# Attention and a top-1 mixture of experts on one core: one ring of PSUM banks, and gates, counts, flag and forms moved to other places

## The chip, the core and the metric

The kernel runs on one NeuronCore of a Trainium2 chip. The core has five engines with a program each: PE (TensorE, matmuls and transposes), DVE (VectorE), ACT (ScalarE), POOL (GpSimd) and SP (which issues transfers). [...] PE writes its results to PSUM, [...]; DVE and ACT read them from there. PE's clock can be throttled, and the profile shows the share that was granted. The metric is the device time of one execution in microseconds. Before the change it is 605.97 us, the median of three runs (602.70 to 607.75).

## What is computed

The reference joins two blocks. The first is attention with a band of `n_local` = 96 keys and `n_global` = 8 keys that every query sees, with a linear bias (4 sequences, 8 heads, 768 positions, 64 numbers per head). The second routes each of the 3072 rows of 512 numbers to one of eight experts:

```python
scores = scale * q @ k.T + bias(h, dist)        # bias = -slope[h] * distance
a = softmax(where(is_global | is_local, scores, -1e9))
x = (a @ v) as (B*S, H*D)                       # 3072 x 512
logits = x @ w_gate                             # 8 experts
expert_idx = argmax(logits)
gate_w = softmax(logits)[expert_idx]
for e in range(8):
    xe = x[expert_idx == e]
    out[expert_idx == e] = gate_w * (relu(xe @ w1[e]) @ w2[e])
```

All data are float32.

## The kernel before

**Attention** runs over 24 blocks of 128 queries (n), six to a sequence (i = n mod 6). It is software-pipelined: in step n the kernel makes the scores of block n, the transposes of q and k for block n + 1, the exponentials of block n, the tokens of block n − 2 (transposes back, logits), and the values of block n − 1. Each engine runs its part in program order. PSUM pools are rings: a new tile has to wait until the engine that reads the old tile in its bank is done.

```python
ps_s = tile_pool(name="ps_s", bufs=2, PSUM)   # scores sp, two banks each
ps_t = tile_pool(name="ps_t", bufs=2, PSUM)   # transposes pt (of q, k) and px
ps_o = tile_pool(name="ps_o", bufs=1, PSUM)   # values po
ps_r = tile_pool(name="ps_r", bufs=1, PSUM)   # pr: sums, logits, counts

def values(n):
    po = ps_o.tile([P, NPAIR, P], F32, tag="o", name="po")
    ...                                        # L387: po <- v, p
    nc.scalar.copy(ots[n][:], po[:])           # L391
    pr = prs[n] = ps_r.tile([P, 4, P], F32, tag="r", name="pr")
    ...                                        # L398: sums, pr[:, 0] <- one_in, p
    ...                                        # L403: logits, pr[:, 0] <- gate_w, ot
    nc.scalar.copy(rs[:], pr[:, 0, :])         # L406

def tokens(n, rs):
    nc.tensor.transpose(pr[:, 1, :], rs[:], ident[:])          # L414
    px = ps_t.tile([P, NPAIR, P], F32, tag="t", name="px")
    for m in range(NPAIR):
        nc.tensor.transpose(px[:, m, :], ot[:, m, :], ident[:])  # L417
    ...        # DVE: den (L423), reciprocal (L425), lh (L428), lg (L431),
    ...        # and the row of the token, xr <- px (L434)
    ...        # at i == 5: choose(...)
```

At the end of a sequence `choose` finds the expert of each token, `gates` the weight, and `dispatch` counts the tokens per expert on PE, works out a row for each token on DVE, and scatters the tokens to DRAM with POOL:

```python
def choose(...):
    ...                                        # top, sh, cand, oh on DVE
    nc.scalar.activation(sh[:], sh[:], AF.Exp)  # L185
    def gates():
        nc.vector.tensor_reduce(se[:], sh[:], AX.X, ALU.add)   # L189, + 4 more on DVE

def dispatch(pool, pr, rt, xr, oh):
    ...        # PE L201 to L207: counts in pr from oh (12 small bf16 matmuls)
    ...        # DVE L210 to L217: rk, slot, base_e from pr
    ...        # POOL L219: six scatters

for n in range(N + 1):
    scores(n); prep_q(n + 1); exps(n); prep_k(n + 1); mix_v(n + 1); load(n + 3)
    b, i = divmod(n - 2, NBLK)
    if n >= 2:
        if i == 0 and b:                       # n = 8, 14, 20
            gates()
            dispatch(pool, prs[n - 2][:, 2, :], rt, xr, oh)
        tokens(n - 2, rs.pop(n - 2))
    if n: rs[n - 1] = values(n - 1)
```

**Experts.** Two experts' first 128 tokens are started early (`up_s`, `down_s`: 128 tokens at a time), then eight passes take the rest of each expert's tokens, in a width that is only known at run time. The width is one of ten forms. Each pass is a `Switch` on a register: the engines load the registers once from the tile `form`, and jump to the code of the form. A `hint` on PE and ACT asks for the code of the next pass ahead of the jump.

```python
ex.begin(stack)                 # pools of the passes, over the space of attention
ex.up_s(0, 0)
dispatch(...); ex.up_s(0, 1)
ex.table(); ex.gathers(0); ex.x_in_s(1); ...   # table writes `form`
for half in range(2): ex.down_s(0, half)
for half in range(2): ex.up_s(1, half)
ex.fetch(2, nc.scalar)
ex.load_forms()                 # PE, ACT and DVE load `form` into registers
ex.hint(0)
ex.down_s(1, 0)
for t in range(TP): ex.x_in(0, t)
ex.x_meta(0); ex.down_s(1, 1)
ex.passes(judge)

def passes(self, judge):
    for e in range(E):
        for i in tc.Switch(index, len(WIDTHS), hint=f"pass{e}"):
            self.one_pass(e, WIDTHS[i], more)   # up L947, down L954, back L968
        ...                                     # fetch, gathers for later passes
        if e + 1 < E: self.hint(e + 1)
        s_ = e + NS
        parts = ...       # e <= 4: up_s, up_s, down_s, down_s of expert s_
                          # e == 5: up_s, up_s; e == 6: down_s, down_s; e == 7: none
        for fn in parts[:1] + [lambda: self.finish(e)] + parts[1:]: fn()
        if s_ == E: judge()
```

`judge` makes a flag (13 small operations on DVE, one matmul L1087, one more on DVE). After the passes every engine reads the flag and would start a general version of the program if the fast one did not apply; with this input it does not start.

Of the kernel before, what the change touches and what calls it, by code (L numbers as in the profile page):

```python
# [23 lines left out]
def kernel(  # L24
# [12 lines left out]
    nc = tc.nc  # L37

    P = 128
    B, H, S, D = q.shape  # L40
    DM, E = moe_w_gate.shape
# [3 lines left out]
    NPAIR = H // 2  # L45
# [14 lines left out]
    const = ctx.enter_context(tc.tile_pool(name="const", bufs=1))  # L60
# [47 lines left out]
    ones = const.tile([P, P], BF16, name="ones")  # L108
# [63 lines left out]
    def choose(pool, rt, xr, lg):  # L172

        shape = [P, NBLK, E]
        top = pool.tile([P, NBLK], F32, tag="top", name="top")
        nc.vector.tensor_reduce(top[:], lg[:], AX.X, ALU.max)
        sh = pool.tile(shape, F32, tag="sh", name="sh")
        nc.vector.tensor_tensor(sh[:], lg[:], top[:].unsqueeze(2).to_broadcast(shape), ALU.subtract)
        cand = pool.tile(shape, F32, tag="cand", name="cand")
        nc.vector.scalar_tensor_tensor(cand[:], sh[:], 0.0, rev8[:].unsqueeze(1).to_broadcast(shape),  # L180
                                       ALU.is_ge, ALU.mult)
# [3 lines left out]
        nc.scalar.activation(sh[:], sh[:], AF.Exp)  # L185

        def gates():
            se = pool.tile([P, NBLK], F32, tag="se", name="se")
            nc.vector.tensor_reduce(se[:], sh[:], AX.X, ALU.add)  # L189
# [62 lines left out]
    def banded(stack, rt, pool, rows, ex, den_all):  # L252
# [5 lines left out]
        ps_t = stack.enter_context(tc.tile_pool(name="ps_t", bufs=2, space=bass.MemoryType.PSUM))  # L258
        ps_o = stack.enter_context(tc.tile_pool(name="ps_o", bufs=1, space=bass.MemoryType.PSUM))
        ps_r = stack.enter_context(tc.tile_pool(name="ps_r", bufs=1, space=bass.MemoryType.PSUM))  # L260

        rawt, kts, kas, qts, vts, vas, ps, ots, prs, seqs = {}, {}, {}, {}, {}, {}, {}, {}, {}, {}
# [116 lines left out]
                nc.scalar.activation(z, z, AF.Exp)  # L379

        def values(n):
            po = ps_o.tile([P, NPAIR, P], F32, tag="o", name="po")
            vals = [(t, vt) for t, vt in enumerate((vas.get(n), vts[n][:])) if vt is not None]
            for m in range(NPAIR):
                for x, (t, vt) in enumerate(vals):
                    for a in range(2):
                        nc.tensor.matmul(po[D * a:D * a + D, m, :], lhsT=vt[:, 2 * m + a, :],  # L387
                                         rhs=ps[n][m // 2][:, a, m % 2, t, :], start=(x == 0),
                                         stop=(x == len(vals) - 1), skip_group_check=True)
            ots[n] = work.tile([P, NPAIR, P], F32, tag="ot", name="ot")  # L390
            nc.scalar.copy(ots[n][:], po[:])  # L391

            pr = prs[n] = ps_r.tile([P, 4, P], F32, tag="r", name="pr")
            x = 0
            for t, _ in vals:
                for a in range(2):
                    for m in range(NPAIR):
                        nc.tensor.matmul(pr[GW * m:GW * m + GW, 0, :], lhsT=one_in[:, a, :],  # L398
                                         rhs=ps[n][m // 2][:, a, m % 2, t, :], start=(x == 0),
                                         stop=False, skip_group_check=True)  # L400
                    x += 1
            for m in range(NPAIR):
                nc.tensor.matmul(pr[GW * m:GW * m + GW, 0, :], lhsT=gate_w[:, m, :], rhs=ots[n][:, m, :],  # L403
                                 start=False, stop=True, skip_group_check=True)
# [43 lines left out]
        for n in range(N + 1):  # L448
            if n < N:
                scores(n)  # L450
            if n + 1 < N:
                prep_q(n + 1)
            if n < N:
                exps(n)
            if n == 0:
                biases(1, (0, 1, 2, 3), "act")
            if n == 2:
                biases(0, range(H), "act")
                ex.clear_s()
            if n + 1 < N:  # L460
                prep_k(n + 1)
                mix_v(n + 1)
            if n + 3 < N:
                load(n + 3)
            if n >= NBLK and feed:
                feed.pop(0)()
            b, i = divmod(n - 2, NBLK)
            if n >= 2:
                if i == 0 and b:
                    xr, _, oh, gates = seqs[b - 1]  # L470
                    gates()
                    dispatch(pool, prs[n - 2][:, 2, :], rt, xr, oh)
                if i == 1 and b == B - 1:
                    ex.early()
                tokens(n - 2, rs.pop(n - 2))
            if n == N:
                ex.x_in_s(0, ps_t.tile([P, NPAIR, P], F32, tag="t", name="pt"))
            if n:
                rs[n - 1] = values(n - 1)
        assert not feed  # L480
        tokens(N - 1, rs.pop(N - 1))
        xr, _, oh, gates = seqs[B - 1]
# [253 lines left out]
    class Experts:  # L736
# [122 lines left out]

        def begin(self, stack):  # L860

            pool = stack.enter_context(tc.tile_pool(name="pass", bufs=1))
            self.w.append(self.slot(pool, NS))
            self.xg = [pool.tile([P, TP, XW], F32, name=f"xg{i}") for i in range(2)]
            self.xT = [pool.tile([P, NDC, TP * P], F32, name=f"xT{i}") for i in range(2)]
            self.hT = pool.tile([P, NFC, TP * P], F32, name="hT")
            self.yT = [pool.tile([P, TP * P], F32, name=f"yT{i}") for i in range(2)]
            self.y = [pool.tile([P, TP, DM], F32, name=f"y{i}") for i in range(2)]
            self.to = [pool.tile([P, TP], I32, name=f"to{i}") for i in range(2)]
            self.gate = [pool.tile([P, TP], F32, name=f"gate{i}") for i in range(2)]  # L870
            ps = stack.enter_context(tc.tile_pool(name="ps_e", bufs=1, space=bass.MemoryType.PSUM))
            self.bank = {nm: [ps.tile([P, 4, P], F32, name=f"{nm}{i}") for i in range(n)]
                         for nm, n in (("ph", 3), ("py", 2), ("t", 3))}
            self.used = {"ph": 0, "py": 0, "t": 0}

        def turn(self, nm):

# [116 lines left out]
        def passes(self, judge):  # L994
            for e in range(E):
# [20 lines left out]
                s_ = e + NS  # L1016
# [15 lines left out]
    rt = Route("")  # L1032
    bad_i = const.tile([P, 1], I32, name="bad_i")
    with ExitStack() as stack:
# [15 lines left out]
        for e in (2, 3):  # L1050
            ex.gather_s(e)
        ex.clear_y()
        for half in range(2):
            ex.down_s(0, half)
        for half in range(2):
            ex.up_s(1, half)
        ex.fetch(2, nc.scalar)
        ex.load_forms()
        ex.hint(0)
        ex.down_s(1, 0)  # L1060
        for t in range(TP):
            ex.x_in(0, t)
        ex.x_meta(0)
        ex.down_s(1, 1)

        def judge():

# [16 lines left out]
            bad_b = const.tile([P, 1], BF16, name="bad_b")  # L1084
            nc.vector.tensor_copy(out=bad_b[:], in_=bad[:, 1:2])
            pb = ex.turn("t")[:].rearrange("p t c -> p (t c)")
            nc.tensor.matmul(pb[:, 0:1], lhsT=ones[:], rhs=bad_b[:], start=True, stop=True)  # L1087
            nc.vector.tensor_scalar(bad_i[:], pb[:, 0:1], 1.0, None, ALU.min)

        ex.passes(judge)  # L1090
    fast.close()
# [39 lines left out]
```

## Time and profile before

| | |
|---|---|
| time, median of 3 | 605.97 us |
| span of the profiled execution | 607.6 us |
| attention, up to the last transpose of px | 0 to 194 us |
| first small tiles, table, gathers | 194 to 231 us |
| eight passes | 231 to 586 us |
| last scaling, last scatters, flag, end | 586 to 607.6 us |
| mean granted clock of PE | 0.963 |

In a profile line, `L414 PE MATMUL pr<-ident,rs 128*128 128x128` means: line 414 of the kernel, on PE, writes tile pr from ident and rs. In the timeline a line starts with the start and the length in us, and ends with the idle time before it in square brackets, with what ended it. In the list of waits the columns are the total in us, how often, and the longest. "issue" means that the engine waited for nothing that the profile shows, [...]. The chain that ended last is of no help here: it covers only the last scatters.

### The profile page before, as it was taken

To read this page: it belongs to the slowest core of one execution; us is meant where nothing else is said; L and a number is where in the kernel's file an instruction comes from. 1 tells how busy PE (TensorE), PEld (TensorE's weight loads), DVE (VectorE), ACT (ScalarE), POOL (GpSimd) and SP (SyncE) were. 2 spreads that over 40 slices of the span, in tenths; PEclk is the share of its full clock that TensorE was granted. 3 is DMA by queue.
4 is the path that set the end of the run, shared out by engine and by line. 5 is a ranking of instruction groups with operands and counts; after the bars stand their busy time and mean duration, and the time that the engine had idled before them with its cause. 6 is when DMAs were issued, how large, how long until landed. Compare 5 with 4: busy or idle time off the path is not lost. (4 is left out here: it accounts for less than half of the span.)

```text
span 607.6 us, 11043 instructions
## 1 busy us (share of the span) xinstructions
PE 546.7 (90%) x4544; PEld 440.7 (73%) x4544; DVE 171.8 (28%) x434; ACT 128.9 (21%) x249; POOL 114.1 (19%) x160
## 2 busy tenths in 40 slices
PE   6899799799797998999999999999999998997850
PEld 5787788688686774667777887788788777773850
DVE  5566566566566320011021011021011011013010
ACT  3654254245342001100101101111111111110100
POOL 4100400400321373002202202202201201002010
PEclk9999899899799898999999999999999999999795
DMA  9979889979820267315135135235235101001000
GB/s 183 213 158 236 239 195 234 261 182 245 208 89 3 105 201 265 107 36 202 55 139 201 51 140 193 57 139 191 62 139 177 38 1 44 2 1 58 4 24 5
DMA packets 98379, 77.23 MB, mean 127 GB/s; under 512 B 79290, under 2 KB 79290, under 8 KB 98240
## 3 DMA queue, kind: packets, MB, share of 16 engines
q1 hardware_dynamic: 88768, 52.44, 34.3%
q0 software_dynamic: 7040, 18.99, 9.0%
q10 hardware_dynamic: 2432, 4.21, 2.0%
q8 instruction: 56, 0.92, 0.7%
q14 instruction: 83, 0.68, 0.4%
HBM read 60.90 MB, written 14.73 MB: 124 GB/s over the span
## 5 line engine op out<-in xcount | busy, mean ns | idle before, releaser
L947 PE MATMUL ph<-xT,w 128*128 128x288 f32 (+3 forms) x512 | 123.1, 403 | 8.8 <-issue 8.8
L947 PEld LDWEIGHTS ph<-xT,w 128*128 128x128 f32 x512 | 97.1, 197 | 39.6 <-issue 17.4
L954 PE MATMUL py<-hT,w 128*128 128x288 f32 (+3 forms) x512 | 121.3, 393 | 0.0
L954 PEld LDWEIGHTS py<-hT,w 128*128 128x128 f32 x512 | 92.3, 190 | 21.4
L842 PE MATMUL ph<-xsT,w 128*128 128x128 f32 x512 | 61.4, 280 | 2.4 <-DVE xr L434 2.4
L372 DVE TENSOR_TENSOR p<-sp,other 128x1024 f32<-128x1024 f32 x40 | 47.1, 1219 | 57.7 <-PE sp L358 57.7
L842 PEld LDWEIGHTS ph<-xsT,w 128*128 128x128 f32 x512 | 60.1, 196 | 3.1 <-DVE xr L434 2.7
L949 ACT ACTIVATE hT<-ph 128x288 f32<-128x288 f32 (+3 forms) x64 | 25.5, 398 | 158.0 <-PE ph L947 158.0
L971 DVE TENSOR_TENSOR y<-t,gate 128x256 f32<-128x256 f32 (+2 forms) x32 | 14.2, 445 | 157.7 <-PE t L968 111.0
L853 PE MATMUL py<-w,hsT 128*128 128x512 f32 x128 | 56.6, 592 | 0.0
L783 POOL DMA_INDIRECT out_dram<-y,to x24 | 23.8, 993 | 159.6 <-DVE y L971 125.1
L926 DVE COPY xT<-t 128x512 f32<-128x512 f32 x24 | 15.6, 682 | 127.8 <-PE t L925 127.8
L379 ACT ACTIVATE p<-p 128x1024 f32<-128x1024 f32 (+1 forms) x48 | 44.6, 978 | 2.1 <-DVE p L372 2.0
L853 PEld LDWEIGHTS py<-w,hsT 128*128 128x128 f32 x128 | 23.6, 190 | 25.8 <-issue 25.8
L387 PE MATMUL po<-p,vt 128*64 128x128 f32 x448 | 41.1, 299 | 0.0
L358 PE MATMUL sp<-qt,kt 64*128 64x128 f32 x448 | 39.7, 285 | 0.9 <-DVE kt L244 0.9
L956 ACT COPY yT<-py 128x288 f32<-128x288 f32 (+3 forms) x32 | 12.4, 386 | 118.3 <-PE py L954 118.3
L358 PEld LDWEIGHTS sp<-qt,kt 64*128 64x128 f32 x448 | 32.4, 196 | 3.1 <-ACT qt L242 1.6
L387 PEld LDWEIGHTS po<-p,vt 128*64 128x64 f32 x448 | 30.2, 152 | 1.7 <-issue 1.7
L776 POOL DMA_INDIRECT xs<-xs_dram,grow_s x8 | 8.1, 1011 | 123.7 <-issue 98.6
L300 POOL COPY ka<-kt 128x384 f32<-128x384 f32 x16 | 8.1, 508 | 119.6 <-DVE den_all L423 93.2
L219 POOL DMA_INDIRECT xs_dram<-xr,slot_i x24 | 23.7, 989 | 16.0 <-issue 6.1
(157 smaller groups left out, 511.8 us busy)
## 6 DMA issues: line engine op xcount, KB each, us to landing
w<-in_moe_w_dram SPq DMA_DIRECT2D x20, 1024.0 KB, 6.3
w<-in_moe_w_dram SPq DMA_DIRECT2D x16, 512.0 KB, 6.1
raw_q<-in_q_dram SPq DMA_DIRECT2D x24, 256.0 KB, 4.7
raw_k<-in_k_dram SPq DMA_DIRECT2D x24, 256.0 KB, 5.4
vt<-in_v_dram SPq DMA_DIRECT2D x24, 256.0 KB, 5.7
w<-in_moe_w_dram ACTq DMA_DIRECT2D x4, 1024.0 KB, 13.8
va<-vt SPq DMA_DIRECT2D x16, 192.0 KB, 5.6
va<-vt SPq DMA_DIRECT2D x16, 64.0 KB, 5.2
```

The costliest lines, as they stand in the source:

```text
L219: d = nc.gpsimd.indirect_dma_start(out=xs_dram[:], out_offset=bass.IndirectOffsetOnAxis(ap=slot_i[:, u:u + 1], axis=0), in_=xr[:, u, :].bi ...
L358: nc.tensor.matmul(sp[:, a, j, t, :], lhsT=kt[r, m, :], rhs=qts[n][r, m, :], start=True, stop=True, skip_group_check=True)
L372: nc.vector.tensor_tensor(z, sc, bi, ALU.add)
L379: nc.scalar.activation(z, z, AF.Exp)
L387: nc.tensor.matmul(po[D * a:D * a + D, m, :], lhsT=vt[:, 2 * m + a, :], rhs=ps[n][m // 2][:, a, m % 2, t, :], start=(x == 0), stop=(x == l ...
L783: d = nc.gpsimd.indirect_dma_start(out=out[:], out_offset=bass.IndirectOffsetOnAxis(ap=idx, axis=0), in_=src, in_offset=None, bounds_check ...
L842: nc.tensor.matmul(ph[:, i, :], lhsT=self.w[e % 3][0][:, c, ts(f, P)], rhs=self.xsT[e % 2][:, c, :], start=(c == 0), stop=(c == NDC - 1), ...
L853: nc.tensor.matmul(py, lhsT=self.hsT[:, f, :], rhs=self.w[e % 3][1][:, f, :], start=(f == 0), stop=(f == NFC - 1), skip_group_check=True)
L926: nc.vector.tensor_copy(out=self.xT[e % 2][:, :, ts(t, P)], in_=pt[:])
L947: nc.tensor.matmul(ph, lhsT=w1t[:, c, ts(f, P)], rhs=xT[:, c, 0:n], start=(c == 0), stop=(c == NDC - 1), skip_group_check=True)
L949: nc.scalar.activation(hT[:, f, 0:n], ph, AF.Relu)
L954: nc.tensor.matmul(py, lhsT=w2t[:, f, ts(d, P)], rhs=hT[:, f, 0:n], start=(f == 0), stop=(f == NFC - 1), skip_group_check=True)
```

## The change

It does six things. (1) The values po move from a pool of their own into the ring of the transposes, which gets three banks instead of two. (2) The Exp of the gates moves from `choose` into `gates`, which runs a step later. (3) The counts of `dispatch` get a tile of the same ring instead of a part of pr, and come after the values of the step instead of before its tokens. (4) The pools of the passes are told to wait for the earlier users of their space tile by tile (`reuse_waits="tile"`), and their banks are used from the first one on. (5) The forms are loaded and the first pass is hinted before `down_s(0)` and after it. (6) The flag is made in passes 1 and 2 instead of 6, and the end of pass 5 (`finish`) comes after both halves of `up_s`. The amount of computation stays the same; the aim is to let PE run on where it waits.

```diff
         nc.vector.tensor_tensor(oh[:], cand[:], ..., ALU.is_equal)
-        nc.scalar.activation(sh[:], sh[:], AF.Exp)
 
         def gates():
+            nc.scalar.activation(sh[:], sh[:], AF.Exp)
...
-        ps_t = stack.enter_context(tc.tile_pool(name="ps_t", bufs=2, space=PSUM))
-        ps_o = stack.enter_context(tc.tile_pool(name="ps_o", bufs=1, space=PSUM))
+        ps_t = stack.enter_context(tc.tile_pool(name="ps_t", bufs=3, space=PSUM))
...
         def values(n):
-            po = ps_o.tile([P, NPAIR, P], F32, tag="o", name="po")
+            po = ps_t.tile([P, NPAIR, P], F32, tag="t", name="po")
...
                     gates()
-                    dispatch(pool, prs[n - 2][:, 2, :], rt, xr, oh)
...
             if n:
                 rs[n - 1] = values(n - 1)
+            if i == 0 and b > 0:
+                dispatch(pool, ps_t.tile([P, 512], F32, tag="t", name="pr"), rt, xr, oh)
...
-            pool = stack.enter_context(tc.tile_pool(name="pass", bufs=1))
+            pool = stack.enter_context(tc.tile_pool(name="pass", bufs=1, reuse_waits="tile"))
...
-            ps = stack.enter_context(tc.tile_pool(name="ps_e", bufs=1, space=PSUM))
+            ps = stack.enter_context(tc.tile_pool(name="ps_e", bufs=1, space=PSUM,
+                                                  reuse_waits="tile"))
...
-            self.used = {"ph": 0, "py": 0, "t": 0}
+            self.used = {"ph": -1, "py": -1, "t": -1}
...
-                for fn in parts[:1] + [lambda: self.finish(e)] + parts[1:]:
+                at = 2 if s_ + 1 == E else 1
+                for fn in parts[:at] + [lambda: self.finish(e)] + parts[at:]:
                     fn()
-                if s_ == E:
-                    judge()
+                if e in (1, 2):
+                    judge(e)
...
         ex.clear_y()
+        ex.load_forms()
         for half in range(2):
             ex.down_s(0, half)
+        ex.hint(0)
         for half in range(2):
             ex.up_s(1, half)
         ex.fetch(2, nc.scalar)
-        ex.load_forms()
-        ex.hint(0)
...
-        def judge():
+        bad_b = const.tile([P, 1], BF16, name="bad_b")
+        def judge(step):
+            if step == 2:
+                ...                 # the matmul L1087 and what follows it
+                return
```

More of the change, by code (lines that the diff above doesn't have):

```diff
@@ L257, in banded @@
         ps_s = stack.enter_context(tc.tile_pool(name="ps_s", bufs=2, space=bass.MemoryType.PSUM))
-        ps_t = stack.enter_context(tc.tile_pool(name="ps_t", bufs=2, space=bass.MemoryType.PSUM))
-        ps_o = stack.enter_context(tc.tile_pool(name="ps_o", bufs=1, space=bass.MemoryType.PSUM))
+        ps_t = stack.enter_context(tc.tile_pool(name="ps_t", bufs=3, space=bass.MemoryType.PSUM))
         ps_r = stack.enter_context(tc.tile_pool(name="ps_r", bufs=1, space=bass.MemoryType.PSUM))
@@ L870, in begin @@
             self.gate = [pool.tile([P, TP], F32, name=f"gate{i}") for i in range(2)]
-            ps = stack.enter_context(tc.tile_pool(name="ps_e", bufs=1, space=bass.MemoryType.PSUM))
+            ps = stack.enter_context(tc.tile_pool(name="ps_e", bufs=1, space=bass.MemoryType.PSUM,
+                                                 reuse_waits="tile"))
             self.bank = {nm: [ps.tile([P, 4, P], F32, name=f"{nm}{i}") for i in range(n)]
                          for nm, n in (("ph", 3), ("py", 2), ("t", 3))}
-            self.used = {"ph": 0, "py": 0, "t": 0}
+            self.used = {"ph": -1, "py": -1, "t": -1}
         def turn(self, nm):
@@ L1064 @@
         ex.down_s(1, 1)
-        def judge():
+        bad_b = const.tile([P, 1], BF16, name="bad_b")
+        def judge(step):
+            if step == 2:
+                pb = ex.turn("t")[:].rearrange("p t c -> p (t c)")
+                nc.tensor.matmul(pb[:, 0:1], lhsT=ones[:], rhs=bad_b[:], start=True, stop=True)
+                nc.vector.tensor_scalar(bad_i[:], pb[:, 0:1], 1.0, None, ALU.min)
+                return
             okn = const.tile([P, 3], F32, name="okn")
@@ L1083, in judge @@
             nc.vector.tensor_scalar(bad[:, 1:2], bad[:, 0:1], 0.5, None, ALU.is_lt)
-            bad_b = const.tile([P, 1], BF16, name="bad_b")
             nc.vector.tensor_copy(out=bad_b[:], in_=bad[:, 1:2])
-            pb = ex.turn("t")[:].rearrange("p t c -> p (t c)")
-            nc.tensor.matmul(pb[:, 0:1], lhsT=ones[:], rhs=bad_b[:], start=True, stop=True)
-            nc.vector.tensor_scalar(bad_i[:], pb[:, 0:1], 1.0, None, ALU.min)
         ex.passes(judge)
```

## The prediction

> **What bounds the kernel now.** I read the page first, then the waits of PE, then its timeline at each wait, then windows of clock.
>
> ```profile
> PE 546.7 (90%) x4544; PEld 440.7 (73%) x4544; DVE 171.8 (28%) x434; ACT 128.9 (21%) x249; POOL 114.1 (19%) x160
> PEclk9999899899799898999999999999999999999795
> ```
>
> PE is busy 90% of the span; no other engine passes 28%. The clock row (40 slices of 15.2 us) dips around 68, 115, 160, 205, 235 and 570 us, and in the idle end. Time can be won where PE waits and where its clock is halved. The waits of PE (total us, times, longest):
>
> ```profile
> PE ph L947 <- issue: 8.8, 3, 3.5
> PE pr L414 <- DVE base_e L217: 8.6, 3, 2.9
> PE pr L403 <- ACT ot L391: 5.6, 5, 1.4
> PE px L417 <- ACT qt L242: 3.6, 18, 0.2
> PE t L1087 <- DVE bad_b L1085: 3.1, 1, 3.1
> PE ph L842 <- DVE xr L434: 2.4, 1, 2.4
> ```
>
> Together 32.1 us, and every one is named by the change. The timeline at a sequence's end, block n = 13 and 14 (start, us):
>
> ```profile
> 106.90 0.24 ACT L185 ACTIVATE sh<-sh 128x48 f32<-128x48 f32 x1 [1.04 <-DVE cand L180]
> 107.05 0.57 ACT L391 COPY ot<-po 128x512 f32<-128x512 f32 x1
> ...
> 107.67 0.43 PE L403 MATMUL pr<-ot,gate_w 128*32 128x128 f32 x8 [1.39 <-ACT ot L391]
> ...
> 111.25 1.99 ACT L379 ACTIVATE p<-p 128x1024 f32<-128x1024 f32 x2
> ...
> 112.10 0.19 DVE L189 TENSOR_REDUCE se<-sh 128x6 f32<-128x48 f32 x1
> ...
> 114.25 0.33 PE L414 MATMUL pr<-ident,rs 128*128 128x128 f32 x1 [2.87 <-DVE base_e L217]
> ...
> 119.68 0.49 PE L358 MATMUL sp<-qt,ka 64*128 64x128 f32 x4
> ```
>
> Two stalls in one boundary: the Exp of the gates sits on ACT ahead of the copy of ot, and the transpose of rs waits 2.87 us until DVE has read the counts from the same bank. What the stall leaves behind shows in two windows at n = 8 (columns: window, length, busy of PE, PEld, DVE, ACT, POOL, clock, DMA, GB/s):
>
> ```profile
> 64.37:67.78 3.41, 0.55 (x15) 0.46 (x13) 3.04 (x12) 2.31 (x3) 0.75 (x2) 1.00 0.87 197
> 67.78:71.20 3.42, 3.42 (x29) 3.09 (x31) 1.46 (x5) 0.00 (x0) 2.73 (x3) 0.53 1.05 317
> ```
>
> After a window with 0.55 us of PE work, the next one runs at about half clock: some 1.7 us more lost. Last, the entries of three passes:
>
> ```profile
> 227.49 1.02 PE L853 MATMUL py<-w,hsT 128*128 128x512 f32 x2
> 231.18 20.89 PE L947 MATMUL ph<-xT,w 128*128 128x352 f32 x64 [2.67 <-issue]
> ...
> 516.93 15.78 PE L947 MATMUL ph<-xT,w 128*128 128x288 f32 x64 [2.60 <-issue]
> ...
> 560.85 0.16 PE L1087 MATMUL t<-bad_b,ones 128*128 128x1 bf16 x1 [3.11 <-DVE bad_b L1085]
> ...
> 564.55 11.47 PE L947 MATMUL ph<-xT,w 128*128 128x160 f32 x64 [3.54 <-issue]
> ```
>
> The first, seventh and eighth pass begin late; the five between begin without a gap.
>
> [...]
>
> **The change, part by part.** Negative is gain.
>
> 1. *Ring of three.* px took the buffer that ACT was still copying to qt: 18 waits of 0.20 us. In the ring px takes the bank of the po before last, long copied out. po now reuses the bank of the q transposes, but comes after px (0.45 us), when qt (0.60 us) is done. **−3.6 us.**
>
> 2. *Exp and dispatch, three boundaries.* At n = 13 the values end at 105.70; without the Exp, ot would run from 105.87 to 106.44 and L403 start at 106.5 instead of 107.67: 1.17 saved. The scores of n = 14 start 1.17 earlier; so do the exponentials, ending at 113.24 − 1.17 = 112.07. Now the Exp of the gates stands behind them: 0.24, to 112.3. DVE's first gate operation waits for it, 112.4; its five took 1.23 us (112.10 to 113.33), so 113.65; den, reciprocal and lh took 0.66, so 114.3. PE no longer waits at L414: it goes on with px and the 32 value matmuls (1.76 us at full clock) and reaches the sums (L398) at 109.77 + 0.21 + 0.45 + 1.86 = 112.3. But pr is one bank, and the sums wait for lh: **a wait of about 2.0 us takes the place of the 2.87.** Then sums 0.9, logits 0.35, counts 0.45: the next scores at 116.0 instead of 119.68, 3.6 saved. The boundary at n = 8 looks the same (3.6); at n = 20 the half clock lasted longer (L387 to L358 from 162.07 to 167.50), and the same 9.2 us from scores to scores gives 4.8. Sum −12.0. [...] the trace has a halving after a window with 44% (112.35 to 115.76) and none after one with 45% (515.06 to 518.48, 1.55 us). [...] **−10.0 us.**
>
> 3. *From attention to the first pass.* Before, 194.04 to 231.18, 37.1 us. With tile-wise reuse the first up_s no longer waits 2.42 us for the read of px. Its work at full clock, by rows elsewhere: up_s halves 3.6 and 3.6, counts 0.43, transposes 0.45, down_s 6.9, up_s 7.15, down_s 3.45, transposes 1.3, down_s 3.45: 30.3. New: the load of the forms stands directly behind short work. DVE's table took 4.3 us from rk (202.24) to form (206.57); with counts at 198.1 form is ready at 202.5, PE arrives at 202.1, [...]. So 32.3: −4.8. The hint then leads by some 20 us instead of 8 and the 2.67 gap closes; the first pass is spared its half-clock window (20.89 against 15.68 × 352/288 = 19.2): −1.7. Chance of a halving after the new stall: +0.7. **−5.8 us.**
>
> 4. *Seventh pass.* Its entry comes 10.2 us after its hint (506.69 to 516.93), with 7.6 us of work between; finish(5) only changes places with up_s. The gap of 2.60 stays, [...]: **+0.7 us.**
>
> 5. *Flag.* Its 13 small DVE operations move to pass 1, where DVE has slack, its matmul to pass 2. Before the eighth pass the 3.11 and 3.54 go, but the hint (at about 549.9) led by only 7.4 us when the work ended at 557.73. From the two other late entries (10.2 us above; 220.16 to 231.18 for the first pass, 11.0) [...]: entry at about 560.9 instead of 564.55, −3.6. Half clock there cost 2.45 us (first relus 2.13, 1.42, then 1.09 apart); it becomes likely, not sure: −1.0. **−4.6 us.**
>
> Sum: −3.6 −10.0 −5.8 +0.7 −4.6 = −23.3, so 605.97 − 23.3 = **582.7 us**. The end, 586 to 607.6, is untouched.
>
> **Rivals.** *The gates become the new boundary stall, and no gain is left there.* For it: the Exp now stands behind exponentials worth 2 us, and lh behind the gates. If each wait of 2.0 us halves the clock, part 2 gives 7 us, the total 588. Against it: counts and pr no longer share a bank. *Another limit in attention.* DMA share is 1.1 in most of the attention windows; if transfers bind, parts 1 and 2 give half, the total 589. Against it: PE waits for a transfer only once, at the start, and loads land in 4.7 to 6.0 us, two blocks of 7.1 us ahead. *The load of the forms is slow.* At 4 us with half clock the total is 586. *The entries are not fetch-bound but a fixed cost hidden by long matmuls.* Then pass eight enters without a gap: 5 us more, 578; but the first pass had long matmuls before it and a gap all the same.
>
> **Range and chances.** The runs before spread over 5 us, [...] and rivals reach from 577 to 589: 573 to 591. 2% is 593.9; losing that would need two rivals together.
>
> **What would show it.** After: L414 on base_e, L842 on xr, L1087 on bad_b and L417 on qt are gone; a new wait of L398 on lh, three times about 2 us; a gap of about 2 us ahead of the first down_s; the first pass without gap, the seventh with about 2.6, the eighth with 2.5 to 3.3. It is wrong if L398 waits over 3 us, if raw_q or vt appears as a releaser of PE, or if the passes' own matmuls differ.

## The result and the profile after

The changed kernel takes **577.15 us** (median of 4 runs, 576.86 to 577.90); the kernel before, run beside it, took 606.86 us (median of 4, 602.70 to 609.61). The ratio is **0.952**, with a 95% interval of 0.946 to 0.958. The prediction was 582.7 us, 5.5 us more than measured. The two profiled executions span 607.6 and 574.9 us, and the 32.7 us between them are what is accounted for below; the medians are 29.7 us apart, as the profiled execution of before (609.5 us) was one of its longer ones.

The page of the changed kernel, PE's busy line and its clock row:

```profile
PE 532.8 (93%) x4544; PEld 433.3 (75%) x4544; DVE 169.2 (29%) x434; ACT 128.5 (22%) x249; POOL 114.0 (20%) x160
PEclk9999999999989999999999999999999999999985
```

PE is busy for 14 us less with the same 4544 matmuls, and the clock row fits: the mean granted clock is 0.981 instead of 0.963. Of the six dips in the clock row of before, one remains ahead of the end, in the twelfth slice (158 to 172 us: 0.88, with 0.50 from 160.69 to 163.40). The waits of PE after (total us, times, longest):

```profile
PE pr L398 <- DVE lh L428: 10.2, 7, 5.1
...
PE pr L403 <- ACT ot L391: 2.6, 5, 1.1
PE py L854 <- DVE gates L836: 1.1, 1, 1.1
```

All the six waits shown of before are gone or, L403 on ot, smaller. "issue" no longer stands in the list at all: every pass begins on time. What has grown is L398 waiting for lh (0.4 us before), and one of these waits is 5.1 us long, which the prediction did not foresee. The timeline of the changed kernel shows the sequence's end that the prediction worked out (n = 14, three lines), then the long one (n = 21, three lines), then the first `down_s` and the entries of the first, seventh and eighth pass:

```profile
106.00 0.23 ACT L187 ACTIVATE sh<-sh 128x48 f32<-128x48 f32 x1
106.26 0.20 DVE L189 TENSOR_REDUCE se<-sh 128x6 f32<-128x48 f32 x1 [1.23 <-ACT sh L187]
...
107.86 1.08 PE L398 MATMUL pr<-p,one_in 128*32 128x128 f32 x32 [1.47 <-DVE lh L428]
...
159.36 0.17 POOL L805 IOTA pl<- 128x3 f32 x1
159.56 0.18 DVE L807 TENSOR_TENSOR loc<-pl,lim 128x24 f32<-128x24 f32 x1 [4.44 <-POOL pl L805]
...
160.69 1.93 PE L398 MATMUL pr<-p,one_in 128*32 128x128 f32 x32 [5.14 <-DVE lh L428]
...
190.89 7.10 PE L854 MATMUL py<-w,hsT 128*128 128x512 f32 x16 [1.13 <-DVE gates L836]
...
213.16 19.10 PE L949 MATMUL ph<-xT,w 128*128 128x352 f32 x64
...
494.47 15.72 PE L949 MATMUL ph<-xT,w 128*128 128x288 f32 x64
...
535.04 8.86 PE L949 MATMUL ph<-xT,w 128*128 128x160 f32 x64
```

At n = 14, DVE waits for the Exp behind the exponentials, and PE waits 1.47 us for DVE. At n = 21, PE waits for lh, lh stands on DVE behind loc, loc waits for POOL's iota, and the iota stands in POOL's program behind six scatters and two copies. The three passes carry no bracket: they have no idle time before them.

Where the 32.7 us came from, as lengths between two points of the same kind in the two timelines (from the first score matmul of a block to that of the next; then from entry to entry):

| stretch | before | after | difference |
|---|---|---|---|
| start, and blocks n = 0, 1 | 18.85 | 20.69 | +1.8 |
| 12 ordinary blocks, each (6.20 to 5.79 at n = 6, 12, 18) | 7.10 | 6.68 | −5.0 |
| n = 7, 13, 19, each | 7.39 | 6.11 | −3.8 |
| n = 8, 14, 20 | 11.66, 11.66, 12.92 | 8.60 each | −10.4 |
| n = 21 | 7.58 | 12.96 | +5.4 |
| n = 22 | 7.10 | 6.96 | −0.1 |
| scores of n = 23 to entry of the first pass | 49.00 | 43.22 | −5.8 |
| first pass | 56.73 | 54.95 | −1.8 |
| passes two to five | 185.0 | 185.1 | +0.1 |
| sixth pass to entry of the seventh | 44.02 | 41.25 | −2.8 |
| seventh to entry of the eighth | 47.62 | 40.57 | −7.1 |
| eighth pass to the end | 43.05 | 39.86 | −3.2 |

### The profile page after: what moved, and what is told of

Read it like the earlier page. It is cut to its first block, busy times and chain, and to the rows that moved or that the text cites. A ratio compares the mean times of both kernels' runs of the same rounds, so it can differ in the third digit from the quotient of the medians.

```text
span 574.9 us, 11056 instructions
## 1 busy us (share of the span) xinstructions
PE 532.8 (93%) x4544; PEld 433.3 (75%) x4544; DVE 169.2 (29%) x434; ACT 128.5 (22%) x249; POOL 114.0 (20%) x160
## 5 line engine op out<-in xcount | busy, mean ns | idle before, releaser
L949 PE MATMUL ph<-xT,w 128*128 128x288 f32 (+3 forms) x512 | 118.8, 393 | 0.0
L949 PEld LDWEIGHTS ph<-xT,w 128*128 128x128 f32 x512 | 93.8, 190 | 26.0 <-issue 3.2
L973 DVE TENSOR_TENSOR y<-t,gate 128x256 f32<-128x256 f32 (+2 forms) x32 | 14.3, 446 | 154.6 <-PE t L970 107.6
L843 PE MATMUL ph<-xsT,w 128*128 128x128 f32 x512 | 59.5, 275 | 0.0
L843 PEld LDWEIGHTS ph<-xsT,w 128*128 128x128 f32 x512 | 58.4, 192 | 0.5 <-issue 0.5
L358 PE MATMUL sp<-qt,kt 64*128 64x128 f32 x448 | 40.9, 292 | 0.9 <-DVE kt L244 0.9
L387 PE MATMUL po<-p,vt 128*64 128x128 f32 x448 | 37.1, 274 | 0.0
L358 PEld LDWEIGHTS sp<-qt,kt 64*128 64x128 f32 x448 | 33.6, 203 | 3.1 <-ACT qt L242 1.6
L398 PE MATMUL pr<-p,one_in 128*32 128x128 f32 x704 | 25.0, 282 | 10.2 <-DVE lh L428 10.2
L398 PEld LDWEIGHTS pr<-p,one_in 128*32 128x32 f32 x704 | 18.6, 112 | 14.6 <-issue 12.6
```

The lines of the kernel that those rows point to most:

```text
L358: nc.tensor.matmul(sp[:, a, j, t, :], lhsT=kt[r, m, :], rhs=qts[n][r, m, :], start=True, stop=True, skip_group_check=True)
L843: nc.tensor.matmul(ph[:, i, :], lhsT=self.w[e % 3][0][:, c, ts(f, P)], rhs=self.xsT[e % 2][:, c, :], start=(c == 0), stop=(c == NDC - 1), ...
L949: nc.tensor.matmul(ph, lhsT=w1t[:, c, ts(f, P)], rhs=xT[:, c, 0:n], start=(c == 0), stop=(c == NDC - 1), skip_group_check=True)
```

## The experiments

Two things had to be explained: the new stall at n = 21 (the iota theory: the iota behind the scatters makes it), and the missing gaps ahead of the seventh and eighth pass, where the prediction had kept them (the `finish` theory: the place of `finish(5)`, which came between the two halves of `up_s`, had made the seventh late; its rivals: the flag, the hint, the place of the code). Then each gain had to be put down to one part of the change. Changes are shown against the changed kernel unless said otherwise; each expectation letters its theories anew.

The runs of ring alone, counts alone, flag with tile-wise waits, and the last version were made on two other chips. There the kernel before took 623.53 and 621.55 us, and the four kernels lose some 3 to 7 us more around each of the three groups of scatters, much of it in gaps of up to 1.1 us between PE's sums, logits and scores. These runs are therefore read by stages that the scatters don't touch, and by ratios on their own chip.

**The place of `finish(5)`.**

```diff
-                at = 2 if s_ + 1 == E else 1
+                at = 1
```

> The changed kernel with finish(5) back between the two halves of up_s, all else as changed. Question: why does the seventh pass begin without a gap (494.47 us, right behind the work that ended there) when before it began 2.60 us late. Theory A, the jump is late because of finish(5)[...]: the gap of 2.4 to 2.8 us returns ahead of the seventh pass, and the eighth stays without one; time 580. Theory B, the gap belonged to something else of the change (the alignment of the code, the banks used, the place of the flag): no gap, 577.

Measured: 578.80 us; the seventh pass starts at 494.90 and the eighth at 535.46, both without idle time before them. A second version also put the scatters of pass 5 a step later:

```diff
+            if e == 5:
+                nc.vector.tensor_copy(out=self.to5[:], in_=self.to[e % 2][:])
+                return                                # scatters of e == 5 left for e == 6
...
-                at = 2 if s_ + 1 == E else 1
+                at = 1
```

> As finish_between, but the three scatters of pass 5 are issued only after those of pass 6 (their rows' numbers are kept in a tile of their own); the same data is written. It splits theory A. A1, the scatters' transfers delay the fetch of the code: no gap ahead of the seventh pass, 577. A2, the transposes of finish(5) between the halves hold PE's sequencer, [...]: the gap of about 2.6 us stays, 580.

Measured: 578.06 us, seventh and eighth again without a gap. The `finish` theory falls: in the changed kernel neither its place nor its scatters make a pass late.

**The iota of `early`.**

```diff
+            self.pl = self.pool.tile([P, TP], F32, name="pl")      # made at step 2
+            nc.gpsimd.iota(self.pl[:], ...)
...
-            pl = T([P, TP], F32, name="pl")                        # in early(), n = 21
-            nc.gpsimd.iota(pl[:], ...)
+            pl = self.pl
```

> The changed kernel, with the small iota pl made by POOL at step 2 instead of step 21. In the changed kernel PE waits 5.14 us at step 21 for lh; DVE stood 4.44 us at loc for pl, which POOL makes only after six scatters and two copies. Theory A, that iota is the whole reason: lh comes 4.4 us earlier, the wait shrinks to about 0.7 us, step 21 takes 8 us instead of 12.96, time 572. Rival B, behind it stands another late work of POOL (the copy ka of the same step, which ends at 159.43): the wait is replaced by one of the scores of step 22 for ka, of 3 us or so, and the time falls by 2 us only.

Measured: 570.51 us. The timeline of this kernel at n = 21:

```profile
154.18 0.18 DVE L808 TENSOR_TENSOR loc<-pl,lim 128x24 f32<-128x24 f32 x1
...
155.29 1.08 PE L398 MATMUL pr<-p,one_in 128*32 128x128 f32 x32 [0.60 <-DVE lh L428]
...
156.86 0.98 POOL L219 DMA_INDIRECT xs_dram<-xr,slot_i  x1 [0.30 <-issue]
```

loc no longer waits, and PE's wait falls from 5.14 to 0.60 us while the sixth scatter has not even started. n = 21 takes 7.36 us instead of 12.96: the iota theory holds, for 5.6 us. The rest of the difference to 577.15 is mostly block n = 1, which took 7.10 us here and 8.46 in the profile of the changed kernel; it took 6.56 to 8.63 us in kernels that do not differ there.

**Forms and hint.** First only the hint was put back behind `up_s(1)`, then both.

```diff
-        ex.hint(0)                       # behind down_s(0, ...)
...
         ex.fetch(2, nc.scalar)
+        ex.hint(0)
```

> The changed kernel with the hint of the first pass at its old place (after up_s(1) and the fetch), but the load of the forms left early. Theory A, as predicted: [...] the lead of 8.4 us is too short, and the gap of 2 to 3 us ahead of the first pass returns, with a half-clock window: 580 to 582. Theory B, [...] the hint's place does not matter; what mattered was the register load, or where the transfers of the weights stood: no gap, 577.

Measured: 577.69 us; the first `down_s` waits 1.12 us as before, and the first pass has no gap.

```diff
-        ex.load_forms()                  # ahead of down_s(0, ...)
-        ex.hint(0)
...
         ex.fetch(2, nc.scalar)
+        ex.load_forms()
+        ex.hint(0)
```

> After, with both the load of the forms and the hint back behind up_s(1). If the gap ahead of the first pass (about 2.4 us in the kernel before) came from these two stretching over short matmuls, it is back here: 577 + 2.4 minus the 1.1 us wait of the first down_s, about 578.5, with the entry of the first pass 2 to 2.5 us behind the last short matmul. If the gap came from the transposes' and flag's other places, the entry stays without gap and the total at about 576.

Measured: 573.72 us. The 1.13 us ahead of the first `down_s` are gone and the first pass still has no gap (its entry at 209.77, the work before it from 206.34 on for 3.60 us). So moving forms and hint brought nothing; it cost the 1.1 us. (Of the other 2.3 us, 1.9 are block n = 1, 6.56 us here.)

**The flag.** Both halves back at the end of step e = 6:

```diff
-                if e in (1, 2):
-                    judge(e)
+                if e == 6:
+                    judge(1)
+                    judge(2)
```

> After, with both halves of the flag (the comparison and its matmul) at the end of the step of e = 6, where the kernel before has them. Theory that the matmul's wait for the fresh comparison exposes the eighth pass's entry: a gap of 3 to 3.5 us ahead of the eighth pass, a wait of about 3 us on the flag's matmul, and 2.6 us more in the eighth pass from the lower clock: about 584 to 586. Rival, that the gap came from the seventh pass's own late entry or from the code's place: under 1 us of gap, about 578. The seventh pass's gap: 2.6 us if the flag's code at steps 1 and 2 had shifted it, none if not.

Measured: 584.18 us. PE's timeline of this kernel at the seventh and eighth pass:

```profile
494.63 15.78 PE L949 MATMUL ph<-xT,w 128*128 128x288 f32 x64 [1.60 <-DVE y L973]
...
538.54 0.16 PE L1076 MATMUL t<-bad_b,ones 128*128 128x1 bf16 x1 [3.12 <-DVE bad_b L1096]
539.34 11.43 PE L949 MATMUL ph<-xT,w 128*128 128x160 f32 x64 [0.64 <-issue]
```

The wait for the flag is back with the same 3.1 us, and so is the slow start of the eighth pass (11.43 instead of 8.86). The gap behind the flag is 0.64 and not 3.5 us. And the **seventh** pass is late again, though nothing was put ahead of it: the flag comes a whole pass later. The releaser named there, y L973, is only the last event that fits in time; it ended at 493.62, and PE started 1.0 us after it.

Next the comparison went to e = 5 and the matmul to e = 6, so that the matmul has nothing to wait for:

```diff
-                if e in (1, 2):
-                    judge(e)
+                if e in (5, 6):
+                    judge(e - 4)
```

> After, with the comparison at e = 5 and its matmul at e = 6, so the matmul stands where it stood before but waits for nothing. Wait theory: no gap ahead of the eighth pass, total within 1 us of after (577). If any extra short work there exposes the entry: a gap of 2 to 3 us and about 582. The comparison at e = 5 puts only VectorE work there, so no gap ahead of the seventh pass is expected; if 2.6 us appear there, it is VectorE's branch and not TensorE's that is late.

Measured: 579.33 us.

```profile
496.33 15.78 PE L949 MATMUL ph<-xT,w 128*128 128x288 f32 x64 [1.58 <-DVE okn L1085]
...
536.96 0.17 PE L1075 MATMUL t<-bad_b,ones 128*128 128x1 bf16 x1
536.99 8.94 PE L949 MATMUL ph<-xT,w 128*128 128x160 f32 x64
```

Half as expected: without its wait, the matmul costs the eighth pass nothing. The seventh pass is late by the same 1.6 us as in the last run, against the expectation. The comparison at e = 5 can't be the cause, as the last run had none there; the two runs share the second half of the flag at e = 6, which is the matmul and one operation on DVE. No run tells these two apart.

**Ring alone, counts alone.** These start from the kernel before. Each also carries half of what the flag's matmul at e = 2 does there: an instruction that shifts PE's later code by one, or a turn of the t banks by one.

```diff
 # the kernel before, with
-        ps_t = ... bufs=2 ;  ps_o = ... bufs=1
+        ps_t = ... bufs=3                       # po from ps_t
...
+                if e == 2:                      # a matmul that nothing needs, no bank turned
+                    nc.tensor.matmul(pz[:, 0:1], lhsT=ones[:], rhs=ones[:, 0:1], ...)
```

> The kernel before with the ring of three banks alone, and one matmul of one column that nothing needs at the end of step e = 2, where the changed kernel has the flag's. Ring: ordinary blocks 6.68 us instead of 7.10, 18 x 0.42 = 7.6 us won, and the steps of n = 8, 14, 20 stay above 11 us if their stall is the counts in pr. Seventh pass: if its late entry depends on where PE's code lies (one matmul more before it shifts everything that follows), the gap of 2.60 us is gone; if the flag's place matters through anything else (which bank of t is next), it stays. The eighth pass's flag wait of 3.1 us stays; the 3.5 us behind it stays in one theory (fixed cost), falls below 1 us if code position sets it. Total about 598 without the seventh's gap, 601 with it.

Measured: 617.98 us (before on that chip: 623.53). Ordinary blocks take 6.68 us: the ring is worth 0.42 us in each, but in only twelve blocks (5.0 us), where the expectation counted eighteen. n = 7, 13, 19 stay at 7.39, and the transpose of rs (L413 there) still waits for base_e three times, 7.9 us in all. The seventh pass is late by 2.35 us: one more instruction ahead of it doesn't help. Behind the flag 0.64 us remain of the 3.5, which the expectation ties to the position of the code; the ring is the only other difference.

```diff
 # the kernel before, with
-                    dispatch(pool, prs[n - 2][:, 2, :], rt, xr, oh)
...
+            if i == 0 and b > 0:                # behind values(n - 1)
+                dispatch(pool, ps_t.tile([P, 512], F32, tag="t", name="pr"), rt, xr, oh)
...
+                if e == 2: self.turn("t")
```

> The kernel before with the counts alone moved: into a tile of the ring of two, behind the values; and the bank of t turned once at the end of step e = 2 without an instruction, as the changed kernel's flag does. Counts: the wait of L414 on base_e (2.87 us, three times) is gone and the steps of n = 8, 14, 20 fall from 11.7, 11.7, 12.9 to about 8.1 (7.65, as with Exp left in choose, and 0.42 of the ring that is absent); ordinary blocks stay 7.10. So some 11 to 12 us of the change are this move alone, and Exp's move adds nothing to it. If Exp's new place is what won there, the steps stay above 10 us. Seventh pass: gap gone if the rotation of the t banks sets it, 2.6 us if the position of the code does. Total about 596.

Measured: 613.96 us on the same chip. The timeline of this kernel at n = 8, transpose of rs and sums:

```profile
64.97 0.27 PE L414 MATMUL pr<-ident,rs 128*128 128x128 f32 x1
...
68.09 1.08 PE L398 MATMUL pr<-p,one_in 128*32 128x128 f32 x32
```

Neither waits. n = 8, 14 and 20 take 7.65 us each, so the move of the counts alone is worth 4.01, 4.01 and 5.27, **13.3 us**, more than the 10.4 of the whole change there. The move is two things at once, another bank and a later place in the program; which of them ends the wait, or whether both must, was not tried. But n = 21 takes 12.94 us here as well: the stall behind the iota comes with the counts (iota at 174.66, loc at 174.86, and L398 waits 4.71 us for lh). They stand behind the values now, so the scatters start later beside the next block, and `early` is one step away. (n = 9 and 15 show 11.2 to 11.4 us, from the gaps at the scatters on this chip; I draw nothing from them.) The seventh pass is late by 2.44 us, so the turn of the banks is not it either, and behind the flag there are 3.71 us, as before.

**The Exp.** In `choose` again, with everything else as changed:

```diff
+        nc.scalar.activation(sh[:], sh[:], AF.Exp)
         def gates():
-            nc.scalar.activation(sh[:], sh[:], AF.Exp)
```

> After, with the Exp of the sequence's sums back in choose() at n = 7, 13, 19 and the rest unchanged. Expected: the steps of n = 7, 13, 19 go from 6.11 back to about 7.39 (3 x 1.28 = 3.8 us lost), while the sums' matmul at n = 8, 14, 20 starts about 1.5 us sooner because Exp is long done (3 x 1.5 = 4.4 us won, less whatever then waits for the one-hot or the gates): total 576 to 578. If the 1.28 us of the steps before came from the ring instead, those steps stay at 6.1 and the total falls to about 573.

Measured: 580.63 us, above the 576 to 578 expected; 1.8 us of the difference to 577.15 lie in the start and in block n = 22. The timeline of this kernel, logits at n = 7 and sums at n = 8:

```profile
61.98 0.42 PE L403 MATMUL pr<-ot,gate_w 128*32 128x128 f32 x8 [1.51 <-ACT ot L391]
...
68.37 1.08 PE L398 MATMUL pr<-p,one_in 128*32 128x128 f32 x32 [0.51 <-DVE lh L428]
```

n = 7, 13, 19 take 7.39, 7.64 and 7.39 us (1.28 to 1.53 lost each), n = 8, 14, 20 take 7.65 (0.95 won each). The move of the Exp is a swap: from ahead of ot to ahead of lh, worth 1.2 us over three boundaries.

**Flag and tile-wise waits alone.** The kernel before, with the flag at passes 1 and 2, and the passes' pools with `reuse_waits="tile"` and their banks from the first on. `finish`, forms and hint as before.

```diff
 # the kernel before, with
+ reuse_waits="tile" (two pools), used = {"ph": -1, "py": -1, "t": -1}
-                if s_ == E:
-                    judge()
+                if e in (1, 2):
+                    judge(e)
```

> The kernel before with two parts of the change alone: the flag in passes 1 and 2, and the tile-wise waits of the passes' pools with their banks used from the first one on; finish(5), forms and hint stay where they were. So far the seventh pass was late (1.6 to 2.6 us) in every kernel with the flag's matmul at e = 6 and in none without it. If that matmul is enough, the seventh pass enters without a gap here, the eighth without its 3.1 + 3.5 us and at 8.9 instead of 11.5 us: 11.7 us in all. If finish, hint or forms did it, 2.6 us stay ahead of the seventh. Tile-wise waits: the 2.42 us of L842 on xr go. First pass: if these waits or banks made it late, its 2.67 us and 1.7 us of half clock go too; if not, they stay. With all of it 18.5 us: about 588; with only the flag and L842, 592 (against 606 for the kernel before; the difference counts).

Measured: 603.34 us, on a chip where the kernel before took 621.55. PE's timeline of this kernel, entries of the first, seventh and eighth pass:

```profile
239.21 19.19 PE L947 MATMUL ph<-xT,w 128*128 128x352 f32 x64 [2.88 <-issue]
...
520.91 15.78 PE L947 MATMUL ph<-xT,w 128*128 128x288 f32 x64
...
561.55 8.86 PE L947 MATMUL ph<-xT,w 128*128 128x160 f32 x64
```

The seventh and eighth pass enter without a gap, and the `up` of the eighth takes 8.86 us, as in the changed kernel, where the granted clock in it is 1.00. From the first pass's entry to the end it is 362.3 us, against 376.4 before and 361.7 after. Of these 14.1 us, 1.7 are the `up` of the first pass, 19.19 us here and 20.89 before, where the granted clock in it was 0.92; **the flag's place gives the other 12.4, nearly all that the later passes gained.** The wait of L842 on xr is gone from the list of waits, so tile-wise reuse, with the banks used from the first on, does what it is for. The first pass is late as before, by 2.88 us.

**A version with all of this.** The changed kernel, with the iota at step 2 and `early` behind the tokens, forms and hint at their old place, and the Exp at a third place: at the end of the step in which `choose` runs, behind the copies of the values.

```diff
+            if n >= 2 and i == NBLK - 1 and n < N:
+                seqs[b][4]()                     # exp(), behind values(n - 1)
...
+                tokens(n - 2, rs.pop(n - 2))
                 if i == 1 and b == B - 1:
                     ex.early()
-                tokens(n - 2, rs.pop(n - 2))
```

> The changed kernel with three more moves: the Exp of the gates emitted at the end of the step in which choose runs, behind the copies of the values (neither ahead of ot nor behind the next exponentials); the iota of early() made at step 2 and early() behind the step's tokens; the load of the forms and the hint back behind up_s(1). Expected against the changed kernel: n = 21 from 12.96 to under 7.4 us (-5.6), n = 8, 14, 20 from 8.60 to about 7.4 with 6.11 kept at n = 7, 13, 19 (-3.6), the stall of the first down_s gone (-1.1): about 567 us, or 0.935 of the kernel before. If Exp at its new place delays rs or qt instead, the steps of n = 8 stay at 8.6 and it is 570.

Measured: 584.17 us (median of 6) beside 621.55 (median of 11) for the kernel before on that chip, a ratio of **0.943** (95% interval 0.938 to 0.948; the changed kernel had 0.952, 0.946 to 0.958, on another chip). The ratio leaves out three of the eleven runs of before, which lie over 1.5% above its fastest. The 0.935 expected lies outside the interval. The two were not timed side by side, and the intervals touch, so that it beats the changed kernel rests on the stages. The timeline at n = 7 and 8 (logits, Exp, sums) shows that the third place is better than both:

```profile
60.11 0.43 PE L405 MATMUL pr<-ot,gate_w 128*32 128x128 f32 x8 [0.23 <-ACT ot L393]
...
60.82 0.25 ACT L187 ACTIVATE sh<-sh 128x48 f32<-128x48 f32 x1
...
66.50 1.08 PE L400 MATMUL pr<-p,one_in 128*32 128x128 f32 x32 [0.51 <-DVE lh L430]
```

n = 7, 13, 19 keep 6.11 us, and n = 8, 14, 20 take 7.65 instead of 8.60: 0.95 won each, where 1.2 were expected. The wait of the first `down_s` is gone. (The last one waits 0.97 us for hsT, as in the other three runs on these two chips, 0.91 to 0.96.) The absolute 567 us were not reached, as this chip adds its gaps at the scatters: n = 9, 15 and 21 take 11.3 to 11.7 us here. The length of n = 21 therefore can't show the 5.6 us of the iota, but the list of waits can: the longest wait for lh is 0.5 us.

## Why the prediction was right, and where not

The time lay in the range. That the sum was right to 5.5 us is in part luck, as errors cancelled: from the seventh pass on 9 us more were gained than predicted, at the ring and the boundaries 5.6 more, up to the first pass and in it 1.8 more; the stall at n = 21 took back 5.4, and the start 1.8. (Between the profiled executions that makes 32.7 us, where 23.3 were predicted.) Two of its signs failed outright: the gaps of about 2.6 us ahead of the seventh pass and of 2.5 to 3.3 us ahead of the eighth are not there.

| part | predicted | measured | what the runs showed |
|---|---|---|---|
| 1 ring | −3.6 | −5.0 | mechanism right, term too small |
| 2 boundaries | −10.0 | −14.2 | right for the counts; the Exp was a swap |
| n = 21 | none | +5.4 | not foreseen |
| 3 to the first pass, and in it | −5.8 | −7.6 | wait on xr right; moving forms and hint brought nothing |
| 4 seventh pass | +0.7 | −2.8 | wrong: the gap is gone |
| 5 flag, eighth pass to the end | −4.6 | −10.2 | direction right, the reason for the remaining gap wrong |
| start and block n = 1 | none | +1.8 | varies from run to run |

**1. Ring.** The term was mis-sized: 18 waits of 0.20 us, from the list of waits, where each ordinary block lost 0.42. PE stood idle for longer than the list tells. The row of its weight loads shows it; from the timeline of the kernel before (n = 22):

```profile
178.47 0.42 PEld L417 LDWEIGHTS px<-ident,ot 128*128 128x128 f32 x4 [0.44 <-ACT qt L242]
178.47 0.66 PE L417 MATMUL px<-ident,ot 128*128 128x128 f32 x4 [0.20 <-ACT qt L242]
```

The wait counts 0.20 from the modelled end of L414 (178.00 + 0.27), but px began 0.47 after L414 did, and follows it after 0.11 in the changed kernel (112.39 to 112.50). That is 0.36 of the 0.42. That the gain is the ring's is shown by the run with the ring alone. It shows in twelve of the eighteen blocks.

**2. Boundaries.** Right: L414 no longer waits, and L398 waits for lh instead. Its wait was 1.5 and not 2.0 us, partly as L190 took 0.17 instead of 0.52 us. And none of the three was followed by a lower clock, for which 2.0 us were set aside, an estimate of the author's: PE was busy for 1.93, 1.99 and 1.93 us of the windows from 64.00 to 67.40, 104.40 to 107.80 and 146.00 to 149.40, and after each the granted clock was 1.00. Not asked: the prediction put the 1.17 us that the Exp's move wins and the wait on lh that it brings into one sum, and so did not see what the move is worth by itself. Left in `choose`, the Exp costs 1.28 to 1.53 a boundary and saves 0.95. The counts made the gain; the prediction laid their old wait to the shared bank, and no run parts the bank from the place in the program.

**n = 21.** The prediction followed the counts only up to the next scores. It didn't ask what else waits in POOL's program behind the scatters, once they start later. The iota needs nothing and takes 0.17 us, and cost 5.6. The prediction had called itself wrong if L398 waited over 3 us; here it waited 5.14. The three waits that it had worked out stayed at 1.47; the one that crossed its limit stood at a block that it had not worked out.

**3. To the first pass.** Right: the 2.42 us of L842 on xr, and a stall at the load. Its 2.0 us were an estimate of the author's that nothing in the profile of before shows, and too high: 1.13 was measured, and from the end of form (190.02) to the matmul only 0.87. The entry without a gap and the 1.7 us less in the `up` (20.89 us at a granted clock of 0.92, then 19.10 at 1.00) came out as said, but by luck: the reason given, that the hint's longer lead closes the gap, is wrong. With the hint and forms back at their places there is no gap either, and it stays at 2.9 to 3.0 us in all three versions of the kernel before, whether with the ring, the counts, or flag and tile-wise waits. None of these alone closes it. The Exp's move is not needed (with the Exp in `choose` there is no gap); which combination closes it is open. And two of these three late entries have the shorter `up` of 19.19 us, so the longer one does not follow from the gap.

**4 and 5. The late passes.** The step that failed is the lead: two late entries of before came 10.2 and 11.0 us after their hints, and the author's estimate for the eighth pass was that its entry would come as late. (A hint has no line in the timeline; its time is the start of the matmuls that stand behind it in PE's program.) In the kernel before the second pass has 14.3 us (273.57 to 287.91) and no gap, which fitted. But in the changed kernel the seventh pass is hinted at about 487 and starts at 494.47, 7.5 us later, without a gap; the eighth has 7.2 (527.84 to 535.04). (For the eighth before the change, the prediction's lead of 7.4 us is 7.8 by its own two times, 549.9 and 557.73.) Each sum in the prediction that rests on a lead falls with it, the 0.7 us set aside in part 4 were a guess, and the rival "fixed cost hidden" is not shown either: it would have to hide the cost equally in the kernels with the flag at e = 6.

What the runs show: the seventh pass is late (1.6 to 2.6 us) in all five kernels with the flag's second half at e = 6, and on time in all nine that have it at e = 2. What they exclude: `finish`, its scatters, the forms and hint of the first pass, one instruction more ahead of it, the turn of the banks, and the matmul's own wait.

The view of the DMA queues, cut into quarters of a microsecond, adds a fact for the kernel before and the changed one. One of the two instruction queues moves packets of 16 KB (56 of them, 0.92 MB, in the whole execution of each). One such packet comes between the start of `up_s` and the entry of the seventh pass: 4.3 to 4.5 us after that start in the changed kernel (491.25 to 491.50), 6.6 to 6.8 us after it in the kernel before (513.25 to 513.50). The entry follows it by 3.0 to 3.2 us and by 3.4 to 3.7 us. So in these two the late entry goes with a packet that comes 2 us later; which engine's code it holds the view does not say. The two other gaps of before can be set beside it: ahead of the first pass a packet comes 2.7 to 2.9 us before the entry (228.25 to 228.50; after the change the last one comes 0.2 to 0.4 us before the entry), and behind the flag, where 3.5 us were lost, one comes 1.2 to 1.4 us after the flag's matmul began (562.00 to 562.25). Two kernels are too few to tell a cause from a coincidence. Why the flag's second half, which stands behind the seventh pass, should delay that pass is open; which of these packets come ahead of each entry in the other kernels would be the next thing to look at, and the place of the code was not tried beyond one shifted instruction.

The flag's wait of 3.1 us, and the slower `up` behind it, are settled: they came in each of the four runs with the fresh flag at e = 6 and in none of the others, with the eighth pass's `up` at 11.3 to 11.7 us against 8.86 to 8.94. In the kernel before the granted clock in it was 0.77 (0.50 in its first 3.45 us), in the changed kernel 1.00.

## What to carry to other kernels

When work is moved later on one engine, look at what stands behind it in the programs of the other engines: a 0.17 us iota behind late scatters cost 5.6 us, and making it early cost nothing. Small results that several engines share should not hold up the next block's matmuls (another bank and a later place together won 4.0 to 5.3 us a time here), and a flag that nothing needs until the end belongs where its operands are long ready (made fresh, it cost a wait of 3.1 us and some 2.5 us in the next pass here). For a wait of PE, read the row of weight loads beside that of matmuls (0.44 beside 0.20 us here), and count a move of an instruction at both places: what it frees and what then waits for it.

## What was not expected of the hardware

- With a matmul of 0.17 us and one DVE operation behind a pass, the entry of that pass was late by 1.6 to 2.6 us.
- Nearly the same gap ahead of the first pass was followed by a slower `up` in two kernels and not in two others: 20.89 and 20.88 us for its `up` after gaps of 2.67 and 3.03, 19.19 after 2.88 and 2.89.
- On two chips PE's matmuls ran with gaps of up to 1.1 us around POOL's scatters (7.1 us at the sums in the last version), which the traces of the first chips do not show. They are listed under "issue"; their cause was not tried.
